# Small transfers on SyncE's queue, Fourier preparation over more slots, and weight decodes asked for earlier, in a one-core attention and MLP kernel

## The chip, the cores and the metric

The kernel runs on one core of a Trainium2 chip. The core has five engines that run side by side, each through its own instructions in order: TensorE (PE in the profile, with its weight loads as PEld), VectorE (DVE), ScalarE (ACT), GpSimd (POOL) and SyncE (SP), which only issues transfers. The metric is the device time of one execution in microseconds (us), lower is better.

## What is computed

Three layers, one behind the other, in float32:

```python
# 1: causal attention with a decay, 4 batches x 8 heads, 576 positions, 64 wide
scores = scale * q @ k^T;  cum = cumsum(log(clip(f)))
scores = where(causal, -1e9, scores + cum[:, None] - cum[None, :])
attn = exp(scores - max);  x = (attn / sum(attn)) @ v          # (4, 576, 512)
# 2: Fourier mixing and an MLP
u = x + real(fft(fft(x, axis=seq), axis=channel))
u = u + relu(norm(u) @ w_ch1) @ w_ch2                           # 512 -> 2048 -> 512
# 3: a second mixing
theta = u @ w_theta;  zr, zi = u * cos(theta), u * sin(theta)
u = u + w_tok_r @ zr + w_tok_i @ zi
out = u + relu(u @ w_ch)
```

The weights of layers 2 and 3 are stored as 64-bit integers and are decoded on the chip into a high and a low float32 part; each product is a sum of three matmuls (high by high, high by low, low by high).

## The kernel before, in words

**Attention (phase 1).** A loop over slots n = -2 to 32, one head a slot. A slot has four quarters q = 0 to 3, and each quarter takes one step of several generators, in a fixed order that is the order of the program on every engine: `least_units` of head n+2 (row minima of the scores; PE L216, L217, L221, DVE L224), `weight_units` of head n (scores again and the exponential: PE L253 to L258, ACT L259), `least_end` of head n+1 in quarter 1 (PE transposes the minima, L234, ACT writes them to `mr`, L236, two transfers put them into row 66 of `q2`), `av_units` of head n-1 (PE L270 into the bank `pt`, of which there is one), `prep_units` of head n+3 (ACT L191, L196, POOL L192, L200, DVE L202, and a transfer of two rows into `kl`), then `rows` (`pair_units`: for each two heads the division by the sums), `norm`, `fft` (`fft_units`: the Fourier transform of one batch, after each eight slots) and `early` (`stash_units`: eight weight blocks are decoded and kept in DRAM). At the slot's end ACT copies `pt` to `x` (`evac_head`, L284), and a transfer sends the row of sums to `zt`. The next slot's L270 can write `pt` only after that copy.

**`pair_units`**: DVE takes the reciprocal of `zt` (L294, L295); `zd` (to DRAM) and `R` (back, over 64 partitions, 288 KB) are two transfers on SP; DVE and POOL multiply `x` by `R` into `XB` and `XA` (L303, L310); a row goes out and another in (L306 to L314); `E` and `O` are their sum and difference (L318, L319). There are three `x` buffers, so the copy of one head waits until `XA` has read the head three before.

**`fft_units`**: the inputs are folded and split into high and low parts (`xx`, `ee`, `oo`, `xh`, `xl`, `eh`, `el`, `oh`, `ol`: L338 to L355), which is called the Fourier preparation here; then six groups of matmuls with an ACT copy and a DVE difference each, then the sums back into `u`.

**MLP (phase 2).** 96 units (g, c, k): four groups g of four weight blocks, six chunks c of 384 positions, four blocks a chunk. Unit n issues `ffn1` of unit n+2 (12 matmuls, L737, ACT L742, DVE L743) and then `ffn2` of unit n (L751). After each quarter of `ffn2`, `later` takes a step of the norm of a later chunk and one step of a decode (`fill`). A decode has six steps: the transfer of a raw block (L543), ACT L563 and L564, DVE L566 and L567, DVE L571 and ACT L576, DVE L578 and POOL L579, POOL L581 and L582. At most two raw blocks are held, and a decode's first step comes eight ticks after its transfer. A block that is needed before its decode is done is finished on the spot (`finish`). The table `todo` says after which unit a block's decode is asked for. In group 3 the 18 blocks of `wtk` for layer 3 are decoded.

**Layer 3 (phase 3)** begins with the chain PE L931, DVE L937 to L955, ACT L948 to L956, POOL L957, on which the matmuls L967 wait.

Transfers are issued by the engine whose name stands in the call: `nc.sync` is SP's queue, `nc.scalar` is ACT, which issues between its own instructions.

## Time and profile before

| | before |
|---|---|
| median of 3 runs | 1139.08 us (1138.71 to 1142.91) |
| profiled execution | 1138.91 us, of which the span from first to last instruction is 1137.1 us |
| busy over the span | PE 90%, PEld 79%, DVE 54%, POOL 45%, ACT 36% |
| mean granted TensorE clock | 0.938 |
| moved by transfers | 81.43 MB, 72 GB/s on average |

The profile is that of one execution. PE is busy for nine tenths of the span, so what the other engines do counts only where PE waits for it, or where PE runs at the lower of its two clock levels (granted clock 0.5, which is 1.2 of 2.4 GHz). A busy share says nothing about that; the waits, the stages and the clock do.

### The profile page before, as it was taken

The page shows a single profiled execution, that of the slowest core. Times are in us where ns is not written, and L with a number is a line of the kernel's source. Part 1 is how long each engine was busy: PE and PEld are TensorE (multiplying, and loading weights), DVE is VectorE, ACT ScalarE, POOL GpSimd, SP SyncE. Part 2 cuts the span into 40 slices and gives each one's busy share as a digit, 9 for nine tenths or more (in the row PEclk, how much of TensorE's full clock was granted, in tenths as well). Part 3 has the DMA queues.
Part 4 walks back from the last instruction along what each step waited for, and adds up shares of the span by engine and source line. Part 5 has one row for each costly group of instructions (what it writes and reads, how often), then busy time and mean ns, then how long its engine had stood idle before and what let it go on. Part 6 is the DMA issues. An engine that isn't in the chain of part 4 may idle for free.

```text
span 1137.1 us, 16339 instructions
## 1 busy us (share of the span) xinstructions
PE 1018.5 (90%) x6112; PEld 903.5 (79%) x6112; DVE 608.6 (54%) x1260; ACT 409.0 (36%) x861; POOL 512.4 (45%) x515
## 2 busy tenths in 40 slices
PE   4998798879989889878799979997999699999998
PEld 2765575647757677778799969996999699999998
DVE  7465656553655554445533534353446766665654
ACT  3454542423443422232322322232233543443422
POOL 5355645362543532454514534353345854444431
PEclk9998898867989988999999989998999799999999
DMA  3463432432220400110212212122341100000001
GB/s 114 130 190 121 166 121 71 134 117 65 86 94 23 159 12 1 37 38 37 75 38 70 79 56 93 67 82 75 116 137 43 42 1 12 32 11 33 12 32 42
DMA packets 33130, 81.43 MB, mean 72 GB/s; under 512 B 9238, under 2 KB 12694, under 8 KB 33052
## 3 DMA queue, kind: packets, MB, share of 16 engines
q1 hardware_dynamic: 26084, 75.87, 20.1%
q0 software_dynamic: 2288, 3.06, 1.2%
q10 hardware_dynamic: 4680, 1.47, 0.6%
q8 instruction: 48, 0.79, 0.3%
q14 instruction: 30, 0.25, 0.1%
HBM read 66.87 MB, written 13.36 MB: 71 GB/s over the span
## 4 chain that ended last, share of the span: by engine, by line
PE 59%; DVE 12%; POOL 8%; ACT 4%; issue 3%; DMA 3%; ACTq 0%; SPq 0%; POOLq 0%; DVEq 0%
PE pa L737 16%; PE pb L751 8%; PE po L751 6%; PE pt L270 4%; PE pb L967 4%; PE pa L978 4%; PE pa L931 3%; PE po L967 2%; PE pa L216 2%; PE pb L253 1%; PE pb L374 1%; PE pb L402 1%; PE pa L217 1%; PE pb L254 1%; POOL a L579 1%
## 5 line engine op out<-in xcount | busy, mean ns | idle before, releaser
L737 PE MATMUL pa<-un,wf 128*128 128x384 f32 x1152 | 228.6, 345 | 31.0 <-ACT wf L576 14.0
L737 PEld LDWEIGHTS pa<-un,wf 128*128 128x128 f32 x1152 | 206.5, 193 | 38.9 <-ACT wf L576 15.0
L743 DVE SCALAR_TENSOR_TENSOR h<-pa,h 128x384 fp32r<-128x384 f32 x96 | 53.5, 557 | 196.4 <-ACT h L742 196.2
L270 PE MATMUL pt<-PT,v 128*65 128x320 f32 (+4 forms) x448 | 122.2, 395 | 22.4 <-ACT x L284 22.4
L751 PE MATMUL pb<-h,wf 128*128 128x384 f32 x636 | 132.7, 341 | 1.4 <-DVE u L759 1.4
L224 DVE TENSOR_REDUCE mn<-pa 128x1 f32<-128x512 f32 (+2 forms) x192 | 84.7, 471 | 79.9 <-PE pa L221 75.1
L742 ACT ACTIVATE h<-pa 128x384 fp32r<-128x384 f32 x96 | 46.9, 490 | 192.1 <-PE pa L737 191.4
L751 PEld LDWEIGHTS pb<-h,wf 128*128 128x128 f32 x636 | 113.5, 190 | 3.1 <-DVE u L759 1.7
L967 PE MATMUL pb<-wtk,z 128*128 128x288 f32 x540 | 99.9, 298 | 10.8 <-ACT z L956 7.7
L216 PE MATMUL pa<-hi 128*128 128x512 f32 (+2 forms) x192 | 93.9, 489 | 16.3 <-ACT mn L156 12.3
L751 PE MATMUL po<-h,wf 128*128 128x384 f32 x492 | 106.8, 347 | 0.0
L259 ACT ACTIVATE PT<-pb 128x512 f32<-128x512 f32 (+1 forms) x128 | 63.7, 500 | 103.0 <-PE pb L256 75.9
L957 POOL TENSOR_TENSOR z<-kra,z 128x256 fp32r<-128x256 f32 x72 | 54.2, 771 | 86.2 <-ACT z L956 86.2
L967 PEld LDWEIGHTS pb<-wtk,z 128*128 128x128 f32 x540 | 82.8, 191 | 11.9 <-ACT z L956 7.9
L579 POOL TENSOR_TENSOR a<-a,wf 128x512 f32<-128x512 f32 x24 | 30.8, 1286 | 135.0 <-DVE t L578 120.7
L751 PEld LDWEIGHTS po<-h,wf 128*128 128x128 f32 x492 | 90.8, 196 | 0.0
L270 PEld LDWEIGHTS pt<-PT,v 128*65 128x65 f32 x448 | 57.5, 152 | 34.9 <-ACT x L284 24.4
L192 POOL TENSOR_TENSOR hi<-raw,hi 64x576 fp32r<-64x576 f32 x31 | 44.3, 1429 | 85.9 <-ACT hi L191 73.7
L217 PE MATMUL pa<-kl,q 66*128 66x512 f32 (+2 forms) x192 | 71.2, 372 | 12.9 <-issue 4.9
L253 PE MATMUL pb<-hi 128*128 128x512 f32 (+2 forms) x192 | 73.4, 389 | 0.3 <-DVE ea L411 0.3
L967 PE MATMUL po<-wtk,z 128*128 128x288 f32 x324 | 70.1, 299 | 0.0
L216 PEld LDWEIGHTS pa<-hi 128*128 128x128 f32 x192 | 42.2, 220 | 33.7 <-issue 18.4
(202 smaller groups left out, 2048.9 us busy)
## 6 DMA issues: line engine op xcount, KB each, us to landing
raw<-in_qk SPq DMA_DIRECT2D x31, 576.0 KB
raw<-in_wf SPq DMA_DIRECT2D x32, 512.0 KB
v<-in_vp SPq DMA_DIRECT2D x16, 325.0 KB
raw<-in_wtk SPq DMA_DIRECT2D x18, 288.0 KB
R<-zd SPq DMA_DIRECT2D x16, 288.0 KB
st_wf<-raw SPq DMA_DIRECT2D x8, 512.0 KB
wf<-st_wf SPq DMA_DIRECT2D x8, 512.0 KB
out<-ob SPq DMA_DIRECT2D x12, 288.0 KB
```

The source lines that it names most:

```text
L216: nc.tensor.matmul(out, hi[:, 1, q], hi[:, 0, a:b], start=True, stop=False)
L217: nc.tensor.matmul(out, q2[0:66, q], kl[0:66, a:b], start=False, stop=not diag)
L224: nc.vector.tensor_reduce(mn[:, col : col + 1], ps[:, off : off + b - a], mybir.AxisListType.X, ALU.min)
L253: nc.tensor.matmul(out, hi[:, 0, k], hi[:, 1, a:b], start=True, stop=False)
L259: nc.scalar.activation(PT[:, 512 * bank : 512 * bank + w], ps[:, 0:w], AF.Exp, scale=-0.125)
L270: nc.tensor.matmul(T[:65, 256 + a : 256 + hi_q], v[:, j, g, :], PT[:, PTOFF[j] + a - 128 * j : PTOFF[j] + hi_q - 128 * j], start=j == 0, s ...
L737: nc.tensor.matmul(ps[:, 0:CH], t[:, l, 128 * d : 128 * d + 128], un[r][:, d], start=n == 0, stop=n == 11)
L742: nc.scalar.activation(h[:, 0], ps[:, 0:CH], AF.Relu)
L743: nc.vector.scalar_tensor_tensor(h[:, 1], ps[:, 0:CH], 0.0, f(h[:, 0]), ALU.max, ALU.subtract)
L751: nc.tensor.matmul(outs[d], t[:, l, 128 * d : 128 * d + 128], h[:, r], start=k % G == 0 and n == 0, stop=k % G == G - 1 and n == 2,)
L957: nc.gpsimd.tensor_tensor(z[:, 1], t, f(z[:, 0]), ALU.subtract)
L967: nc.tensor.matmul(acc[k][th], z[:, l, 128 * k : 128 * k + 128], self.wtk[kt][:, r, 288 * th : 288 * th + 288], start=first and i == 0 and ...
```

## The change

Three parts, by what the code does:

1. The four small transfers of the attention that ACT issued (`kl`, two of `mr`, `zt`) are issued by SP. The two of `mr` come a quarter later, the one of `zt` in the next slot's first quarter (`send_sums`).
2. `pair_units` and `fft_units` have their steps in more quarters (two pairs can be under way, `chains`); the last pairs and transforms of batches 2 and 3 take fewer (`tight`). Copies `yh` and `zh` go from ACT to DVE, one difference (`ol`) from POOL to DVE. The early decode takes 12 quarters a block in place of nine.
3. In phase 2 the decodes of a group are asked for at its start, five steps are taken a unit in place of four, and in group 3 eight in place of six, with a wait of six ticks in place of eight.

```diff
-            nc.scalar.dma_start(f(kl[64:66]), f(self.scr[n]))
+            nc.sync.dma_start(f(kl[64:66]), f(self.scr[n]))
...
-        nc.scalar.dma_start(f(q2[66:67, 0:512]).rearrange("o (i s) -> o i s", i=4), f(mr[0:4]))
-        nc.scalar.dma_start(f(q2[66:67, 512:576]), f(mr[4:5, 64:128]))
+        yield
+        nc.sync.dma_start(f(q2[66:67, 0:512]).rearrange("o (i s) -> o i s", i=4), f(mr[0:4]))
+        nc.sync.dma_start(f(q2[66:67, 512:576]), f(mr[4:5, 64:128]))
...
-        nc.scalar.copy(x, T[:65, 256:832])
-        nc.scalar.dma_start(zt[64 * g : 64 * g + 64, :], x[64:65, :].rearrange("o (p c) -> o p c", c=9))
+        self.nc.scalar.copy(hd["x"], T[:65, 256:832])
+    def send_sums(self, hd, zt):
+        self.nc.sync.dma_start(zt[64 * g : 64 * g + 64, :], hd["x"][64:65, :].rearrange("o (p c) -> o p c", c=9))
...
+        self.send_sums(hds[1], zt)
-        for _ in range(2):
+        for _ in range(1 if tight else 2):
             yield
         nc.vector.tensor_scalar(zt, zt, 1e-9, None, ALU.add)
         nc.vector.reciprocal(zt, zt)
+        if not tight:
+            yield
         nc.sync.dma_start(zd, zt)
+        if not tight:
+            yield
...
-        for _ in range(4):
+        for _ in range(3):
             yield
         nc.vector.tensor_tensor(XB[p : p + 64, t, :], hds[1]["x"][0:64], R[:, 1], ALU.mult)
+        nc.gpsimd.tensor_tensor(XA[p : p + 64, t, :], hds[0]["x"][0:64], R[:, 0], ALU.mult)
+        if not tight:
+            yield
...
-        for _ in range(9):
+        for _ in range(6 if tight else 11):
             yield
...
         nc.vector.tensor_tensor(ee[:, :, 1:288], E[:, :, 1:288], E[:, :, 575:288:-1], ALU.add)
         nc.vector.tensor_copy(ee[:, :, 0:289:288], E[:, :, 0:289:288])
+        yield
         nc.scalar.copy(eh, ee)
-        yield
         nc.vector.tensor_tensor(oo[:, :, 0:287], O[:, :, 1:288], O[:, :, 575:288:-1], ALU.subtract)
+        nc.vector.tensor_copy(xx[:, 0:289:288], x256[:, 0:289:288])
+        yield
         nc.scalar.copy(oh, oo)
+        nc.scalar.copy(xh, xx)
...
-        nc.gpsimd.tensor_tensor(ol, oo, f(oh), ALU.subtract)
+        nc.vector.tensor_tensor(ol, oo, f(oh), ALU.subtract)
...
-            nc.scalar.copy(yh[:me, s, :], ps[:me, 0:258])
+            nc.vector.tensor_copy(yh[:me, s, :], ps[:me, 0:258])
...
-        for _ in range(4 if w is self.w2 else 1):
+        for _ in range(3 if w is self.w2 else 1):
             yield
...
-            if self.queue and self.ticks - self.born[self.queue[0]] >= 8:
+            if self.queue and self.ticks - self.born[self.queue[0]] >= self.age:
...
-        for j, (c, k) in enumerate([[1, 3], [2, 3], [4, 2], [4, 3]]):
+        for j, (c, k) in enumerate([[1, 3], [1, 3], [4, 2], [4, 2]]):
             at(0, c, k, load, 4 + j)
         for g in (1, 2):
-            for j, (c, k) in enumerate([[0, 1], [1, 3], [3, 1], [4, 3]]):
-                at(g, c, k, load, G * g + 4 + j)
+            for j in range(4):
+                at(g, 0, 1, load, G * g + 4 + j)
         for j in range(4):
-            at(1, j, 2, self.keep_big, "wth", j)
-            at(2, j, 2, self.keep_big, "wch", j)
+            at(1, 0, 1, self.keep_big, "wth", j)
+            at(2, 0, 1, self.keep_big, "wch", j)
...
-            self.fill(2 if g == 3 and d % 2 else 1)
+            self.fill(2 if g == 3 or d == 1 else 1)
...
+            if g == 3:
+                self.age = 6
```

What the change does to the order on the engines is shown at three places. Lines of the changed kernel are up to 31 higher (L260 is L259 before, L585 is L563, L600 is L576, L771 is L742).

The first is ACT in slot 11, in which the preparation of the first Fourier transform stands; before:

```order
L259 ACTIVATE PT<-pb 128x512
L190 DMA kl_105<-scr 2x576
L191 CAST hi<-raw 128x576
L259 ACTIVATE PT<-pb 128x512
L236 ACTIVATE mr<-pa 5x128
L237 DMA q_99<-mr 1x4x128
L238 DMA q_99<-mr 1x16x4
L196 ACTIVATE hi<-raw 128x576
L342 CAST xh<-xx 1x290
L259 ACTIVATE PT<-pb 128x512
L349 CAST eh<-ee 128x580
L259 ACTIVATE PT<-pb 128x64
```

and in the changed kernel, a slot later, where its preparation stands:

```order
L260 ACTIVATE PT<-pb 128x512
L191 CAST hi<-raw 128x576
L260 ACTIVATE PT<-pb 128x512
L236 ACTIVATE mr<-pa 5x128
L196 ACTIVATE hi<-raw 128x576
L357 CAST eh<-ee 128x580
L260 ACTIVATE PT<-pb 128x512
L361 CAST oh<-oo 128x576
L362 CAST xh<-xx 1x290
L260 ACTIVATE PT<-pb 128x64
L283 COPY x<-pt 65x576
```

The three transfers are gone from ACT, and the copy of `xx`, which depends on the longest chain, went from first to last of the three.

The second is SP in one even slot and the odd one behind it, where before it had:

```order
L296 DMA zd<-zt 128x9
L298 DMA R<-zd 64x1152
L181 DMA raw<-in_qk 128x1152
L587 DMA st_wf_1_1014<-raw 128x1024
L306 DMA rb<-XB 1x576
L314 DMA XB<-rb 1x576
L543 DMA raw<-in_wf 128x1024
L181 DMA raw<-in_qk 128x1152
L176 DMA v<-in_vp 128x650
```

and now, from `R` on to the next `zd`:

```order
L305 DMA R<-zd 64x1152
L238 DMA q_102<-mr 1x4x128
L239 DMA q_102<-mr 1x16x4
L614 DMA st_wf_0_800<-raw 128x1024
L181 DMA raw<-in_qk 128x1152
L176 DMA v<-in_vp 128x650
L190 DMA kl_105<-scr 2x576
L316 DMA rb<-XB 1x576
L287 DMA zt<-x 64x1x9
L565 DMA raw<-in_wf 128x1024
L325 DMA XB<-rb 1x576
L238 DMA q_99<-mr 1x4x128
```

SP's queue now has the small transfers between the large ones (`R`, the raw blocks, the stores `st_wf`), ahead of some and behind others.

The third is ACT at the end of group 1 of phase 2. L742 is the activation of one `ffn1`; what stands between two of them is the decodes' share of one unit. Before:

```order
L742 ACTIVATE h<-pa 128x384 x3
L563 ACTIVATE a<-raw 128x512
L564 ACTIVATE t<-raw 128x512
L576 CAST wf<-a 128x512
L742 ACTIVATE h<-pa 128x384
L563 ACTIVATE a<-raw 128x512
L564 ACTIVATE wf<-raw 128x512
L576 CAST wf<-a 128x512
L563 ACTIVATE a<-raw 128x512
L564 ACTIVATE wf<-raw 128x512
L576 CAST wf<-a 128x512
L742 ACTIVATE h<-pa 128x384
```

and now:

```order
L771 ACTIVATE h<-pa 128x384 x3
L585 ACTIVATE a<-raw 128x512
L586 ACTIVATE t<-raw 128x512
L585 ACTIVATE a<-raw 128x512
L586 ACTIVATE t<-raw 128x512
L771 ACTIVATE h<-pa 128x384
L600 CAST raw<-a 128x512 x2
L771 ACTIVATE h<-pa 128x384 x7
```

Before, two decodes of the block that the next `ffn1` reads stand whole between two activations; now the last weight block (tile `wf`) was decoded ten units earlier, the last rows are blocks for layer 3 (tile `raw`), and seven units follow with no decode.

## Rows read from the trace of the kernel before

**Rows 1.** Stages by windows: phase 1, its end to group 1, groups 1 to 3, layer 3's start.
```profile
core 0: us, PE busy (x) PEld busy (x) DVE busy (x) ACT busy (x) POOL busy (x), PEclk, DMA share, GB/s
45.80:392.80 347.00, 307.25 (x1741) 218.42 (x1741) 196.26 (x399) 147.41 (x301) 170.14 (x149) 0.89 0.36 111
392.80:545.50 152.70, 132.22 (x694) 120.21 (x694) 71.19 (x142) 44.59 (x93) 63.10 (x59) 0.93 0.10 37
545.50:884.70 339.20, 314.08 (x1753) 311.43 (x1753) 156.01 (x311) 100.65 (x200) 144.63 (x130) 0.96 0.25 80
884.70:912.00 27.30, 17.41 (x115) 16.55 (x114) 20.09 (x48) 13.79 (x36) 22.84 (x32) 0.75 0.07 22
```

**Rows 2.** Waits of PE over the span: us in total, times, longest us.
```profile
PE pt L270 <- ACT x L284: 22.4, 13, 3.5
PE pa L737 <- ACT wf L576: 14.0, 3, 5.6
...
PE pa L737 <- POOL wf L582: 9.7, 3, 3.8
PE pb L967 <- ACT z L956: 7.7, 1, 7.7
```

**Rows 3.** Windows, columns as in rows 1: first chunk of each group, and a quiet one.
```profile
545.50:571.50 26.00, 19.28 (x98) 18.63 (x98) 14.56 (x22) 6.68 (x12) 15.79 (x12) 0.87 0.27 82
571.50:588.20 16.70, 16.70 (x98) 16.70 (x97) 6.97 (x15) 4.96 (x10) 0.00 (x0) 1.00 0.08 28
655.20:683.70 28.50, 19.98 (x99) 19.15 (x98) 11.33 (x23) 7.39 (x13) 10.60 (x9) 0.82 0.19 56
...
768.60:796.70 28.10, 19.59 (x98) 18.77 (x97) 10.94 (x22) 7.40 (x13) 10.18 (x9) 0.82 0.24 76
```

**Rows 4.** The page's group of POOL's first decode operation, L579, in phase 2.
```profile
L579 POOL TENSOR_TENSOR a<-a,wf 128x512 f32<-128x512 f32 x24 | 30.8, 1286 | 135.0 <-DVE t L578 120.7
```

**Rows 5.** Windows: a quiet slot, the three preparation slots, and the stretch behind the second.
```profile
53.30:60.80 7.50, 7.50 (x50) 5.50 (x50) 3.64 (x12) 4.05 (x8) 3.58 (x4) 1.00 0.77 222
126.60:141.60 15.00, 9.43 (x52) 6.05 (x50) 10.16 (x20) 6.69 (x13) 10.89 (x11) 0.82 0.41 146
224.90:242.40 17.50, 9.80 (x54) 6.31 (x52) 13.99 (x23) 5.91 (x13) 11.11 (x12) 0.80 0.17 55
323.20:337.40 14.20, 9.60 (x54) 6.15 (x53) 8.79 (x19) 5.49 (x11) 7.14 (x9) 0.89 0.22 67
242.40:277.70 35.30, 34.33 (x138) 25.12 (x139) 11.82 (x28) 11.95 (x27) 9.23 (x9) 0.57 0.29 86
```

**Rows 6.** Timeline of ACT in the first preparation slot: start, us, idle before and releaser.
```profile
135.71 0.43 ACT L342 CAST xh<-xx 1x290 fp32r<-1x290 f32 x1 [3.19 <-DVE xx L341]
...
138.81 0.68 ACT L349 CAST eh<-ee 128x580 fp32r<-128x580 f32 x1 [2.18 <-DVE ee L348]
```

**Rows 7.** Timeline of ACT in slot 5 (q marks the issue of a transfer).
```profile
82.46 0.66 ACTq L237 DMA_DIRECT2D q<-mr  x1
83.17 0.53 ACTq L238 DMA_DIRECT2D q<-mr  x1
83.74 0.68 ACT L196 ACTIVATE hi<-raw 128x576 fp32r<-128x576 f32 x1 [1.31 <-issue]
```

**Rows 8.** ACT's groups in phase 1: the first of the early decode's two conversions.
```profile
L563 ACT ACTIVATE a<-raw 128x512 f32<-128x512 f32 x8 | 5.3, 666 | 0.0
```

**Rows 9.** Timelines: SP's `zd` and the `R` that waits for it; PE's reader of `mr`.
```profile
77.31 0.33 SPq L296 DMA_DIRECT2D zd<-zt  x1
78.92 0.46 SPq L298 DMA_DIRECT2D R<-zd  x1
...
86.88 0.39 PE L254 MATMUL pb<-q,kl 67*128 67x512 f32 x1
```

**Rows 10.** Timelines: one `R` on SP, and DVE's reader of it.
```profile
198.26 0.46 SPq L298 DMA_DIRECT2D R<-zd  x1
...
202.11 0.75 DVE L303 TENSOR_TENSOR XB<-x,R 64x576 f32<-64x576 f32 x1 [0.35 <-DMA R<-zd]
```

More of the change, by code (lines that the diff above doesn't have):

```diff
@@ L309, in pair_units @@
             nc.sync.dma_start(self.x256, row)
-        nc.gpsimd.tensor_tensor(XA[p : p + 64, t, :], hds[0]["x"][0:64], R[:, 0], ALU.mult)
+        if not tight:
+            yield
         if h == 0:
@@ L319, in pair_units, with fft_units @@
             nc.gpsimd.tensor_tensor(O[:, t, :], XA[:, t, :], XB[:, t, :], ALU.subtract)
-        yield
-    def fft_units(self, b, E, O, rows):
+    def fft_units(self, b, E, O, rows, tight):
         nc = self.nc
         w = self.c1
-        for _ in range(9):
+        for _ in range(6 if tight else 11):
             yield
@@ L339, in fft_units @@
         nc.gpsimd.memset(xx[:, 288:290], 0.0)
-        nc.gpsimd.tensor_tensor(xx[:, 1:288], x256[:, 1:288], x256[:, 575:288:-1], ALU.add)
-        nc.vector.tensor_copy(xx[:, 0:289:288], x256[:, 0:289:288])
-        nc.scalar.copy(xh, xx)
-        nc.gpsimd.tensor_tensor(xl, xx, f(xh), ALU.subtract)
         nc.gpsimd.memset(ee[:, :, 288:290], 0.0)
         nc.gpsimd.memset(oo[:, :, 286:288], 0.0)
+        nc.gpsimd.tensor_tensor(xx[:, 1:288], x256[:, 1:288], x256[:, 575:288:-1], ALU.add)
         yield
@@ L348, in fft_units @@
         nc.vector.tensor_copy(ee[:, :, 0:289:288], E[:, :, 0:289:288])
+        yield
         nc.scalar.copy(eh, ee)
+        nc.vector.tensor_tensor(oo[:, :, 0:287], O[:, :, 1:288], O[:, :, 575:288:-1], ALU.subtract)
+        nc.vector.tensor_copy(xx[:, 0:289:288], x256[:, 0:289:288])
         yield
-        nc.vector.tensor_tensor(oo[:, :, 0:287], O[:, :, 1:288], O[:, :, 575:288:-1], ALU.subtract)
         nc.scalar.copy(oh, oo)
+        nc.scalar.copy(xh, xx)
         nc.gpsimd.tensor_tensor(el, ee, f(eh), ALU.subtract)
         yield
-        nc.gpsimd.tensor_tensor(ol, oo, f(oh), ALU.subtract)
+        nc.vector.tensor_tensor(ol, oo, f(oh), ALU.subtract)
+        nc.gpsimd.tensor_tensor(xl, xx, f(xh), ALU.subtract)
         yield
-        if b < B - 1:
+        if not tight:
             yield
@@ L385, in fft_units @@
                 nc.tensor.matmul(ps[:mo, 0:256], l, r, start=k == 0, stop=k == 5)
-            nc.scalar.copy(zh[:mo, s, :], ps[:mo, 0:256])
+            nc.vector.tensor_copy(zh[:mo, s, :], ps[:mo, 0:256])
             nc.vector.tensor_tensor(zl[:mo, s, :], ps[:mo, 0:256], f(zh[:mo, s, :]), ALU.subtract)
@@ L488, in phase1 @@
                 if q == 1 and 0 <= n + 1 < NH:
-                    self.least_end(heads[n + 1])
+                    e = self.least_end(heads[n + 1])
+                if q > 0:
+                    next(e, 0)
                 next(c, 0)
                 next(prep, 0)
-                next(rows, 0)
+                if q == 0 and sums:
+                    self.send_sums(*sums)
+                    sums = None
+                for r in chains:
+                    next(r, 0)
                 next(norm, 0)
@@ L502, in phase1 @@
             if m >= 0:
-                self.evac_head(heads[m], T, zt)
-                if g == 1:
-                    for _ in rows:
-                        pass
-                    rows = self.pair_units(h, (heads[m - 1], heads[m]), zt, XA, XB, E, O, zd, rb)
+                self.evac_head(heads[m], T)
+                b = p // NP
+                tight = b > 1 and h == NP - 1
+                if g == 0:
+                    sums = (heads[m], zt)
+                else:
+                    rows = self.pair_units(h, (heads[m - 1], heads[m]), zt, XA, XB, E, O, zd, rb, tight)
+                    chains.append(rows)
                     if h == NP - 1:
@@ L510, in phase1 @@
                             pass
-                        fft = self.fft_units(p // NP, E, O, rows)
+                        fft = self.fft_units(b, E, O, rows, tight)
+        for _ in chains[0]:
+            pass
         pinned.close()
@@ L575, in decode @@
             self.nraw -= 1
+        if w is self.w2:
+            yield
         nc.scalar.copy(hi, a)
@@ L586, in decode @@
             self.stash[keep] = self.sdram.tile([128, 2, n], F32R, name=name)
+            if w is self.w2:
+                yield
+                yield
             nc.sync.dma_start(f(self.stash[keep]).rearrange("p t n -> p (t n)"), f(flat[:, 0 : 2 * n]))
+            if w is self.w2:
+                yield
         yield
@@ L642, in fill @@
                     self.queue.insert(min(self.active - 1, len(self.queue)), g)
-                    if self.ticks - self.born[self.queue[0]] < 8:
+                    if self.ticks - self.born[self.queue[0]] < self.age:
                         self.queue.remove(g)
@@ L660, in p2_open @@
         self.active = 3
-        self.born, self.ticks = {}, 0
+        self.born, self.ticks, self.age = {}, 0, 8
         for k in range(G):
@@ L684, in norm_units @@
         nc.gpsimd.tensor_tensor(s1, s1, s2, ALU.add)
-        for _ in range(2):
+        for _ in range(3):
             yield
```

15 lines of the change are left out of this document (7 added, 8 removed).

## The prediction, made before the changed kernel ran

> **What bounds the kernel now.** I read the stages first, then the waits of PE, then single slots and units. In the stages [rows 1] the column to read is PE's busy time against the window's length, with the granted clock beside it. Phase 1 takes 347.0 us with PE busy 307.25, so PE waits for 39.75 us of it. Its clock is 0.89, and since the clock has the two levels 0.5 and 1.0, it stood at half for 0.22 x 347 = 76 us. Part of that half-clock time is idle already counted; I take 60 of the 76 us as busy, and half of that, 30 us, as lost. So phase 1 loses about 70 us to waits and to the clock that they bring down. The stretch behind it loses 20.5 us of waiting in 152.7, groups 1 to 3 lose 25.1 us of waiting at a clock of 0.96, and the start of layer 3 waits 9.9 of its 27.3 us. Against these stands the rest of the span, where PE is busy at full clock. PE is the bound, and what can be won is its waits and its half-clock stretches.
>
> The waits say who is late [rows 2]. The largest in phase 1 is L270 behind ACT's copy of `pt`: 22.4 us in 13 waits. In phase 2 three waits for a cast (14.0 us) and three for POOL's last decode operation (9.7 us) stand before an `ffn1`: few and long. One wait of 7.7 us stands at layer 3's start.
>
> The three pairs in phase 2 lie at the group changes [rows 3]. A quiet chunk of 98 matmuls takes 16.70 us; the first chunks of groups 1, 2 and 3 take 26.00, 28.50 and 28.10 with the same 98. That is 9.3 + 11.8 + 11.4 = 32.5 us, the half clock (0.87, 0.82, 0.82) included.
>
> In phase 1 the worst slots are those with a Fourier preparation [rows 5]. A quiet slot takes 7.5 us; these take 15.0, 17.5 and 14.2 with nearly the same matmuls (52 to 54 against 50, for which I allow 0.2 us each slot). The excess is 46.7 - 3 x 7.7 = 23.6 us. Behind the second, 35.3 us run at a clock of 0.57: 86% of it, 30 us, at half, with PE busy for almost all of it, so about 15 us more. Why ACT is late there is seen in its timeline [rows 6]: it stands 3.19 us before the copy of `xx` and 2.18 us before that of `ee`, both waiting for DVE, and the exponentials and the copy of `pt` are queued behind.
>
> **The change part by part.** The sum is made against the profiled execution, 1138.91 us (1137.1 us of span and 1.8 us around it), which is 0.2 us under the median shown.
>
> *Decodes asked for at a group's start, five steps a unit.* In the order on ACT the last two decodes of group 1 stood whole between two activations, so an `ffn1` waited for all their steps. They now stand ten units ahead of it, and what is last are blocks that only layer 3 needs. Groups 2 and 3 then begin without a wait: -11.8 and -11.4 us. In group 1 the blocks can't be asked for earlier than before chunk 4, since their buffers open there; the last one's cast stands just before its `ffn1`. Behind a cast come three POOL operations of 1.29 us [rows 4], 3.9 us, with about 1.5 us for the activation, the cast and a vector operation ahead of them; PE has half a unit of cover, 2.1 us (a unit is 16.70 / 4 [rows 3]). I leave 3.5 us there, with a little half clock: -5.3 in place of -9.3. Together **-28.5 us**. Bounds: -32.5 if that one goes as well, -20 if denser decodes cost DVE and POOL time elsewhere (POOL's 1.29 us three times for each decode, 5 of 6 steps a unit, is 3.2 us of 4.2).
>
> *Eight steps a unit in group 3, six ticks.* Before, four of the eighteen `wtk` decodes remain when `ffn1` has ended, and ACT, DVE and POOL do them inside the first chain of layer 3. In the changed order only the casts of the last two remain. Layer 3's start loses 9.9 us of waiting and, at a clock of 0.75, about 3 us more [rows 1]. The chain itself still has to run once, for which I leave 3 us: **-10 us**, bounds -13 and -4.
>
> *The Fourier preparation over more quarters.* Each ACT copy now stands a quarter, 1.9 us of a 7.5 us slot, behind the DVE or POOL operation that it reads; the waits there are 3.19 and 2.18 us [rows 6], so most of each is covered. ACT also loses the `yh` and `zh` copies to DVE, which was waiting for them. The excess of the three slots and the half clock behind the second is 23.6 + 15 = 38.6 us. I take three quarters of it, **-29 us**, since DVE and POOL operations in these slots are also stretched. Bounds: -38 and -10.
>
> *Transfers off ACT.* The two issues of `mr` take 0.66 and 0.53 us, and ACT's next operation had 1.31 us of idle before it [rows 7]; the other two transfers cost at most as much each, so ACT gets back up to 2.6 us of a 7.5 us slot. With that the copy of `pt` is less late, and the pair division, the decodes' POOL operations and the stores on SP no longer meet in one quarter. The rest of phase 1's loss is 70 - 38.6 = 31 us, spread over some ten waits with different releasers. I take two fifths: **-13 us**. Bounds: -25 and 0.
>
> *A wait that is added.* The early decode now has a fixed rhythm of three slots, and its two conversions on ACT, L563 and L564, always stand in the last quarter, just ahead of the copy of `pt` for which PE waits. Each takes 0.67 us [rows 8] (I take the second as long). About 0.5 us of the 1.3 is covered by what PE does before L270; eight blocks make 8 x 0.8 = **+6 us**. Bounds: 0, and +14 if the raw block is not there yet either, since its transfer is issued in the first quarter of the same slot.
>
> *The small transfers behind the large ones.* `mr` is issued by 83.70 at the latest before [rows 7] and read at 86.88 [rows 9], 3.2 us later. A small transfer's issue to its release of the next takes 1.6 us (77.31 to 78.92 [rows 9]), so 1.6 us are left over. On SP, `R` or a raw block or both may be ahead of it. A quiet slot moves 222 GB/s with the 16 engines busy for 0.77 [rows 5], so 288 GB/s at full; the 288 + 512 KB of both are 2.8 us, about at the margin, and they come together in four slots. I cost this at 0; bounds 0 and +12. The Trainium skill (DMA: Bandwidth & Descriptors, Queues, rings and completion order) says that an engine takes turns between queues, but works through one queue in order. By that rule `mr` gives up its turn beside the bulk when it leaves ACT's queue, and the sum would get the +12; no row here shows it, since ACT issued `mr` in every slot.
>
> *`R` a quarter later.* Its reader now comes three quarters, 5.6 us, behind its issue, where one `R` took 3.85 us (198.26 to 202.11 [rows 10]). Cost 0; what it hides behind is the slot's own matmuls. If it came 1 us late in each of sixteen pairs, `XA` and with it the copy of `pt` would be late, +16.
>
> *The stretch from 392.8 to 545.5.* The transform of batch 3 starts a few steps earlier, and the decodes meet the norms as before: -2 us, bounds -10 and +8.
>
> Sum: -28.5 - 10 - 29 - 13 + 6 - 2 = -76.5. 1138.9 - 76.5 = **1062 us**. With each term at its own distance from the bounds the sum moves by some 20 us either way, so the forecast's own range is 1040 to 1084.
>
> **The rivals.**
>
> *Phase 1 gives little back.* Stalls of this phase have many releasers (for L270, in 13 waits, never over 3.5 us), and taking away one uncovers the next; the added wait and late `R` come in. Then the decode parts stay, -38.5 us, and phase 1 nets nothing: 1100 us. For it: DVE and POOL have the most work in just these slots (13.99 and 11.11 of 17.5 us [rows 5]). Against it: ACT has 2.6 us a slot more.
>
> *More goes than I take.* If phase 1's other waits mostly vanish too and the clock stays up, another 25 us: 1037 us.
>
> *SP's queue becomes the bound: slower.* SP works in order; a transfer that waits for DVE or POOL (`zd`, the stores) holds `mr` behind it, and with `mr` the scores of the next slot. It decides when PE loses 76.5 / 30 = 2.6 us in each of 30 slots, so when `mr` lands 2.6 + 1.6 = 4.2 us later than before. At 3 us a slot, +90: 1152 us. For it: six small transfers a slot now share a queue with up to three large ones. Against it: each of them is placed behind its source by a quarter or more.
>
> *It does not do what it says.* Engines other than PE already carry the decodes with little room, so that asking earlier only moves the waits into the units, and phase 1's waits into other quarters: 1130 to 1140 us. Against it: in the quiet chunk [rows 3] POOL does nothing and DVE 6.97 of 16.70 us.
>
> **How the numbers follow.** Forecast 0.60; little from phase 1 0.18; more than I take 0.11; slower 0.06; nothing 0.05. About 0.5% (6 us) is what a measurement of this kernel can tell from no change. Faster by more than that: 0.60 + 0.18 + 0.11 + 0.02 of the last = 0.91; the same 0.03; slower 0.06. The range takes in the forecast, the better case and most of the first rival: 1032 to 1104 us, 0.60 + 0.11 + 0.12.
>
> **What would show it.** In the profile after: no wait of an `ffn1` for a cast or POOL at the second and third group change, and chunks of 16.7 us there; one short one at the first. L967's wait at layer 3's start at about 3 us. Preparation slots near 9 us, and no 30 us at half clock behind the second. ACT's idle before L196 gone. L270's waits behind the copy of `pt` left mainly in the eight slots with L563 and L564 in the last quarter. I would be wrong if L254 waits for `mr` in many slots, if POOL's `XA` waits for `R` each pair, or if phase 2's units each grow beyond 4.2 us.

## The result and the profile after

The changed kernel takes 1092.78 us (median of 4 runs, 1088.11 to 1093.09) beside 1140.99 us for the kernel before on the same chip (4 runs, 1138.71 to 1148.19): a ratio of 0.956, 95% interval 0.951 to 0.961. The prediction was 1062 us with a range of 1032 to 1104. The direction and the range held; the gain was 48 us where 76.5 had been summed. The medians and ranges below leave out executions more than 1.5% above the fastest of their kernel.

The stages of the changed kernel, by windows with the columns and the order of [rows 1]:

```profile
45.30:377.60 332.30, 305.05 (x1762) 218.82 (x1761) 211.19 (x423) 140.56 (x286) 170.97 (x149) 0.91 0.40 122
377.60:527.50 149.90, 128.28 (x672) 114.97 (x673) 77.32 (x148) 41.26 (x83) 59.48 (x56) 0.94 0.07 24
527.50:850.43 322.93, 310.80 (x1753) 308.02 (x1752) 166.62 (x327) 105.09 (x213) 154.96 (x142) 0.98 0.26 86
850.43:865.90 15.47, 13.82 (x109) 13.37 (x108) 11.87 (x30) 8.72 (x21) 13.13 (x20) 1.00 0.01 2
```

The stages shrank by 14.7, 2.8, 16.3 and 11.8 us; together 45.6 of the 46.1 us by which the span did (1137.1 to 1091.0). Phase 1 hides something here, since the big layers' first `ffn1` runs inside its window: it starts at 360.8 us instead of 389.1, 28.3 us earlier, but the second chunk only at 389.1 instead of 405.0, 15.9 us earlier. So 12.4 us were won and given back within one chunk.

PE's waits over the span, as in [rows 2] (L271 was L270, L766 was L737, L998 was L967, L780 is `ffn2`):

```profile
PE pt L271 <- ACT x L283: 7.4, 10, 1.7
PE pb L732 <- POOL s L727: 6.6, 4, 2.5
...
PE pa L766 <- POOL wf L606: 4.9, 1, 4.9
PE po L780 <- ACT x L283: 4.9, 1, 4.9
PE po L780 <- ACT h L771: 4.3, 2, 2.9
...
PE pa L766 <- ACT wf L600: 1.9, 1, 1.9
...
PE pb L255 <- DMA q<-mr: 1.6, 1, 1.6
PE pb L998 <- ACT z L987: 1.5, 1, 1.5
```

The copy of `pt` costs a third of what it did, and the casts and POOL operations ahead of `ffn1` are down from three each to one. Two rows are new: `ffn2` waits 4.9 us for a copy of phase 1, and 4.3 us for its own activation `h`.

The first chunks of groups 1, 2 and 3, with a quiet one third, as in [rows 3]:

```profile
527.50:553.80 26.30, 19.14 (x98) 18.18 (x97) 11.29 (x20) 6.65 (x12) 15.43 (x12) 0.87 0.23 80
637.60:659.40 21.80, 18.75 (x97) 18.18 (x96) 7.75 (x16) 5.07 (x10) 7.68 (x6) 0.92 0.35 116
659.40:676.10 16.70, 16.70 (x99) 16.70 (x98) 7.15 (x15) 5.42 (x10) 2.52 (x2) 1.00 0.17 56
742.70:761.50 18.80, 17.28 (x97) 16.70 (x97) 7.75 (x16) 5.08 (x10) 7.71 (x6) 1.00 0.31 107
```

Group 1 begins no better than before (26.00), group 2 wins 6.7 us and group 3 9.3, and both still stand 5.1 and 2.1 us over a quiet chunk.

The slots with a Fourier preparation (the first, second and fifth row), the slots behind the second and the third, in which the last of the preparation and the first of the transform now lie (third and sixth), and the stretch behind the second pair (fourth), columns as in [rows 5]:

```profile
136.40:148.00 11.60, 8.91 (x53) 6.23 (x52) 11.50 (x15) 5.35 (x11) 10.41 (x8) 0.90 0.42 127
219.60:228.90 9.30, 7.28 (x48) 5.09 (x46) 9.16 (x17) 5.88 (x14) 5.96 (x5) 1.00 0.38 98
228.90:242.20 13.30, 12.66 (x63) 9.40 (x64) 7.96 (x20) 3.89 (x8) 7.57 (x7) 0.74 0.32 110
242.20:277.50 35.30, 34.68 (x222) 25.25 (x220) 26.20 (x54) 13.43 (x27) 16.49 (x12) 1.00 0.31 93
299.50:308.50 9.00, 8.01 (x51) 5.46 (x50) 8.90 (x15) 5.61 (x11) 6.29 (x5) 1.00 0.32 104
308.50:327.10 18.60, 15.48 (x80) 11.46 (x80) 11.06 (x23) 3.94 (x9) 9.67 (x9) 0.72 0.14 46
```

The preparation slots take 11.6, 9.3 and 9.0 us, near the 9 that was expected (15.0, 17.5 and 14.2 before). The third's gain moved on, since the slot behind it takes 18.6 us where it took 11.2; with the slot behind each, the six take 73.8 us, against 88.1 before. The stretch behind the second pair does 222 matmuls at full clock where 138 ran at 0.57 before.

### The profile page after: what moved, and what is told of

Read it like the earlier page. It is cut to its first block, busy times and chain, and to the rows that moved or that the text cites. A ratio compares the mean times of both kernels' runs of the same rounds, so it can differ in the third digit from the quotient of the medians.

```text
span 1091.0 us, 16375 instructions
## 1 busy us (share of the span) xinstructions
PE 1005.8 (92%) x6112; PEld 892.5 (82%) x6112; DVE 631.1 (58%) x1288; ACT 398.3 (37%) x837; POOL 511.1 (47%) x511
## 5 line engine op out<-in xcount | busy, mean ns | idle before, releaser
L766 PE MATMUL pa<-un,wf 128*128 128x384 f32 x1152 | 229.6, 345 | 18.7 <-ACT un L751 5.3
L766 PEld LDWEIGHTS pa<-un,wf 128*128 128x128 f32 x1152 | 205.0, 192 | 29.0 <-ACT un L751 9.6
L780 PE MATMUL pb<-h,wf 128*128 128x384 f32 x636 | 131.1, 340 | 0.6 <-DVE u L788 0.6
L271 PE MATMUL pt<-PT,v 128*65 128x320 f32 (+4 forms) x448 | 118.7, 386 | 7.6 <-ACT x L283 7.4
L260 ACT ACTIVATE PT<-pb 128x512 f32<-128x512 f32 (+1 forms) x128 | 64.3, 504 | 168.0 <-PE pb L257 141.1
L771 ACT ACTIVATE h<-pa 128x384 fp32r<-128x384 f32 x96 | 46.9, 490 | 197.6 <-PE pa L766 197.4
L780 PEld LDWEIGHTS pb<-h,wf 128*128 128x128 f32 x636 | 113.3, 190 | 1.6 <-DVE u L788 1.3
L780 PE MATMUL po<-h,wf 128*128 128x384 f32 x492 | 105.5, 344 | 9.6 <-ACT x L283 4.9
L998 PE MATMUL pb<-wtk,z 128*128 128x288 f32 x540 | 98.2, 295 | 2.3 <-ACT z L987 1.5
L780 PEld LDWEIGHTS po<-h,wf 128*128 128x128 f32 x492 | 89.5, 193 | 11.5 <-ACT x L283 5.2
L998 PEld LDWEIGHTS pb<-wtk,z 128*128 128x128 f32 x540 | 81.5, 188 | 2.9 <-ACT z L987 1.7
L603 POOL TENSOR_TENSOR a<-a,wf 128x512 f32<-128x512 f32 x24 | 31.3, 1306 | 96.7 <-DVE t L602 96.7
L271 PEld LDWEIGHTS pt<-PT,v 128*65 128x65 f32 x448 | 56.3, 149 | 18.5 <-ACT x L283 9.5
L998 PE MATMUL po<-wtk,z 128*128 128x288 f32 x324 | 69.0, 294 | 0.0
```

Source lines behind the costliest of these rows:

```text
L260: nc.scalar.activation(PT[:, 512 * bank : 512 * bank + w], ps[:, 0:w], AF.Exp, scale=-0.125)
L271: nc.tensor.matmul(T[:65, 256 + a : 256 + hi_q], v[:, j, g, :], PT[:, PTOFF[j] + a - 128 * j : PTOFF[j] + hi_q - 128 * j], start=j == 0, s ...
L766: nc.tensor.matmul(ps[:, 0:CH], t[:, l, 128 * d : 128 * d + 128], un[r][:, d], start=n == 0, stop=n == 11)
L771: nc.scalar.activation(h[:, 0], ps[:, 0:CH], AF.Relu)
L780: nc.tensor.matmul(outs[d], t[:, l, 128 * d : 128 * d + 128], h[:, r], start=k % G == 0 and n == 0, stop=k % G == G - 1 and n == 2,)
L998: nc.tensor.matmul(acc[k][th], z[:, l, 128 * k : 128 * k + 128], self.wtk[kt][:, r, 288 * th : 288 * th + 288], start=first and i == 0 and ...
```

## Where the lost part of the gain went, in the trace

The end of phase 1, by timelines of SP, ACT, DVE, POOL and PE in the changed kernel:

```profile
354.19 0.35 SPq L301 DMA_DIRECT2D zd<-zt  x1
356.29 9.50 SPq L620 DMA_DIRECT2D wf<-st_wf  x8
365.83 0.50 SPq L287 DMA_DIRECT2D zt<-x  x1
366.38 0.62 SPq L305 DMA_DIRECT2D R<-zd  x1
...
375.51 0.75 DVE L310 TENSOR_TENSOR XB<-x,R 64x576 f32<-64x576 f32 x1 [1.03 <-DMA R<-zd]
375.55 1.96 POOL L311 TENSOR_TENSOR XA<-x,R 64x576 f32<-64x576 f32 x1 [6.49 <-DMA R<-zd]
377.55 0.64 ACT L283 COPY x<-pt 65x576 f32<-65x576 f32 x1 [3.66 <-POOL XA L311]
378.24 2.29 PE L780 MATMUL po<-h,wf 128*128 128x384 f32 x6 [4.87 <-ACT x L283]
```

Read it upwards. `ffn2` waits for the copy that frees its PSUM bank; the copy waits for `XA`, which still reads the buffer of `x`; `XA` waits for `R`; and `R` is issued behind eight fetches of 512 KB and lands 9.1 us after its issue, where the one in [rows 10] took 3.85. The Trainium skill (DMA: Bandwidth & Descriptors, Queues, rings and completion order) says that a DMA engine works through the descriptors of one queue in order; the 9.1 us agree, and run e5 tests it. `R` is also issued late, 12.2 us behind `zd`, and part of that is a wait that stands ahead of it on SP: the second of the fetches waits for DVE, by SP's waits from 354 to 367 us:

```profile
SPq L620 <- DVE un L752: 5.8, 1, 5.8
```

Before, `R` was issued ahead of the fetches (379.83 and 382.16 us).

Group 2's first chunk, by timelines of ACT and PE:

```profile
634.70 0.67 ACT L585 ACTIVATE a<-raw 128x512 f32<-128x512 f32 x1 [6.84 <-DMA raw<-in_wth]
...
641.10 0.66 ACT L585 ACTIVATE a<-raw 128x512 f32<-128x512 f32 x1 [5.17 <-DMA raw<-in_wth]
...
642.21 0.48 ACT L771 ACTIVATE h<-pa 128x384 fp32r<-128x384 f32 x1
642.74 1.21 PE L780 MATMUL po<-h,wf 128*128 128x384 f32 x3 [2.90 <-ACT h L771]
```

A decode's conversion stands at the head of ACT's order with its raw block not there. SP had issued that load late (637.38), because it waited for the store of the kept block that used the buffer before (issued at 630.38). Behind the conversion on ACT is the activation that `ffn2` needs.

## The experiments

Of all kernels below those whose orders agree up to there tell how much one execution of phase 1 varies. From the third copy of `pt` to the 31st it takes 290 to 305 us in six traces of the changed order (296.9, 291.0, 290.2, 305.1, 296.3, 293.0) and 323.2 and 329.1 in two of the order before. A phase-1 difference under some 10 us in one trace therefore proves nothing. The experiments ran on other chips than the result; the kernel before took 1139.73 to 1145.17 us there, so a difference to the changed kernel of under some 5 us isn't told by the medians, and where the ratio intervals overlap (e3, e5, e6, e7) the trace has to decide.

**e1: the decodes alone.** In the kernel before:

```
-for j, (c, k) in enumerate([[1, 3], [2, 3], [4, 2], [4, 3]]):
+for j, (c, k) in enumerate([[1, 3], [1, 3], [4, 2], [4, 2]]):
...
-self.fill(2 if g == 3 and d % 2 else 1)
+self.fill(2 if g == 3 or d == 1 else 1)
```

> The kernel before with the decode scheduling of the big layers alone (where loads and keeps are asked for, two steps of decode at d == 1, age 6 in the last group); phase 1 as before. Theory A, the two halves of the change are independent and add: group changes about -16 us and the start of layer 3 about -12 us, so about 1140 - 28 = 1112 us, with layer 3's start at clock 1.0. Theory B, part of the gain of the decodes needs the earlier phase 1 (a clock that is not pulled down, queues that are free): the gain is 20 us or less, 1120 us or more.

Measured: 1116.67 us beside 1139.73, ratio 0.980 (0.976 to 0.984), 23 us. The first chunks take 27.1, 20.1 and 18.9 us (1.1 us lost, 8.4 and 9.2 won, 16.5 in all, against 15.7 in the full change), and layer 3's start, from its first matmul to the next batch of L933 behind L969, takes 15.8 us as in the full change, against 26.4 before. In these stages the decode parts are worth what they are worth in the full change. The time lies between the two theories; this execution's phase 1 was 6 us longer than that of the kernel before, with the same order.

**e2: phase 1 alone.** The same lines put back in the changed kernel.

> The changed kernel with the decode scheduling of the big layers put back to the old one; transfers, preparation and pair division as changed. Theory A (they add): about -18 us, so about 1122 us, group 1 starts near 527 us and the first-chunk stalls of the groups are those of before (7.3 and 10.3, 9.9 and 10.2, 9.9 and 9.8 us units). Theory B: phase 1 alone gives 25 us or more, 1115 us or less, and the new decode order costs something in the stretch before group 1.

Measured: 1132.51 us, ratio 0.992 (0.988 to 0.997), 7 us. So the halves don't add: 23 + 7 is 30, not 48, and neither theory gave this. The missing 18 us stand in one stretch, from chunk 1 of group 0 to group 1, by windows of e2 and of the changed kernel:

```profile
384.40:540.70 156.30, 133.46 (x624) 119.97 (x625) 72.95 (x141) 38.09 (x78) 54.22 (x52) 0.84 0.06 21
```
```profile
389.10:527.50 138.40, 117.50 (x624) 104.50 (x625) 75.22 (x143) 38.12 (x78) 54.85 (x52) 0.96 0.07 24
```

The same 624 matmuls are busy for 133.5 us at a clock of 0.84 and for 117.5 at 0.96; waiting differs by 2 us only (22.8 and 20.9). Behind it are longer single waits, by the waits of PE in that stretch of e2 and of the changed kernel:

```profile
PE pb L732 <- POOL s L727: 12.9, 4, 5.0
```
```profile
PE pb L732 <- POOL s L727: 6.6, 4, 2.5
```

In e2 two POOL operations of a decode (L603, 1.27 us each) stand between the normalisation's sums. A stretch at half clock begins in or at the end of each of the two waits of 5 us and lasts 10.2 and 6.8 us. That is a third of the 50 us that a clock of 0.84 makes in 156.3 us (11 us at 0.96 in the changed kernel), so these waits account for a part only; what starts the rest isn't shown. The change also has one step more ahead of the mean's matmul in the normalisation, which the diff ahead of the prediction doesn't show; e10 takes it out.

**e3: only `mr` back on ScalarE's queue.**

```
-nc.sync.dma_start(f(q2[66:67, 0:512])...)
-nc.sync.dma_start(f(q2[66:67, 512:576]), f(mr[4:5, 64:128]))
+nc.scalar.dma_start(f(q2[66:67, 0:512])...)
+nc.scalar.dma_start(f(q2[66:67, 512:576]), f(mr[4:5, 64:128]))
```

> The changed kernel with only the two mr rows sent from ScalarE's queue again, in the same quarter. Theory A, the mr rows wait behind the bulk transfers of SyncE's queue (R, raw) and that starts the half clock at 70 us: the 1.6 us wait of L255 for q<-mr goes, the 17 us at half clock from 70.5 us shrink to 7 or less, and the kernel is 4 to 10 us faster than the changed one (1083 to 1089). Theory B, the copy of pt, late behind the decode's conversions on ScalarE (1.05 us at 71.2 us), starts it: the wait of L255 goes but the half clock stays, and the time moves by less than 3 us.

Measured: 1097.32 us, ratio 0.963 (0.960 to 0.967): no gain. L255 waits for `mr` 3.9 us in five waits, against 1.6 in one. Theory A falls, and the wait doesn't go, as both theories had it. The long half clock at 70 us, on which both rested, doesn't belong to the order: the slot takes 13.2, 8.9, 8.8, 13.2, 11.1 and 11.3 us in the six traces of the same order. By windows, in the changed kernel and in e2:

```profile
71.20:84.40 13.20, 12.53 (x45) 8.89 (x46) 5.21 (x14) 4.32 (x10) 4.16 (x5) 0.50 0.34 75
```
```profile
72.50:81.30 8.80, 8.13 (x45) 5.74 (x46) 4.38 (x12) 4.32 (x10) 3.72 (x5) 0.81 0.37 88
```

**e4: the early decode's conversions behind the copy of `pt`.**

```
-for _ in range(3 if w is self.w2 else 1):
+for _ in range(4 if w is self.w2 else 1):
...
-    yield
     yield
 nc.sync.dma_start(f(self.stash[keep])...)
```

> The changed kernel with the early decode's two conversions a quarter later (four yields after the raw load, one fewer ahead of the store, so the same 12 quarters a block): they follow the copy of pt instead of standing ahead of it. Theory A (the copy waits behind conversions that wait for raw, the prediction's added wait): the copy-to-copy times of the slots in which a block starts drop by about 1 us each plus the half clock at 70 us, so 6 to 12 us less than the changed kernel (1081 to 1087). Theory B, mr behind the bulk transfers is what starts the half clock: 3 us or less.

Measured: 1103.07 us (1101.71 to 1114.06, three executions), ratio 0.971 (0.965 to 0.977), 10 us slower than the changed kernel. Both theories fall: PE's waits for the copy grow. The waits between the third copy of `pt` and the 31st, first in e4, then in the changed kernel (ACT's for `XA`, PE's for the copy):

```profile
ACT x L283 <- POOL XA L311: 21.2, 7, 4.9
...
PE pt L271 <- ACT x L283: 18.8, 11, 2.6
```
```profile
ACT x L283 <- POOL XA L311: 11.8, 6, 3.8
...
PE pt L271 <- ACT x L283: 7.4, 10, 1.7
```

In the five other traces of the changed order these waits are 12.0 to 13.3 and 6.7 to 9.6 us, so the growth is clear of chance. The copy is late here behind `XA` on POOL, whose buffer it overwrites: in three pairs of e4 the decode's last POOL operation stands directly ahead of `XA`, in the changed kernel in none. With it the edit moved the whole decode, and what the two conversions alone cost ahead of the copy isn't shown. Nor is every late copy behind `XA`: in e11 and e12 PE waits 20 us for the copies and ACT 8 for `XA`.

**e5: the eight fetches behind `R`.** The loads move from the opening of the big layers' pools to the quarter after the sums and `R`:

```
-for k in range(G):
-    self.load(k)
...
 next(fft, 0)
+if n == NH and q == 0:
+    for k in range(G):
+        self.load(k)
```

> The changed kernel with the eight fetches wf<-st_wf of the last slot of phase 1 issued behind R of the pair before the last, instead of ahead of it (the first fetch about 2.5 us later). Theory A (the fetches on SyncE's queue hold up R, whose reader XA holds up the copy that closes phase 1): R lands before 362 us on the changed kernel's scale instead of 375.5, the 4.9 us wait of the first ffn2 matmul for ACT x goes, with the half clock behind it, and the time falls by 5 to 12 us (1081 to 1088). Theory B (the first ffn1 units are bound by the normalisation and by the fetches themselves, which now come later): the first ffn1 waits 2 to 3 us more for wf and the time moves by less than 3 us.

Measured: 1083.04 us (1078.15 to 1093.92), ratio 0.952 (0.943 to 0.961), 9.7 us less than the changed kernel. By timelines of SP, ACT and POOL:

```profile
351.29 0.54 SPq L305 DMA_DIRECT2D R<-zd  x1
351.93 6.69 SPq L623 DMA_DIRECT2D wf<-st_wf  x8
...
360.72 0.62 ACT L283 COPY x<-pt 65x576 f32<-65x576 f32 x1
...
361.87 1.41 POOL L311 TENSOR_TENSOR XA<-x,R 64x576 f32<-64x576 f32 x1
```

`XA` waits for nothing any more and PE's wait behind the last copy is gone. From the first `ffn1` to the second chunk 17.6 us pass, against 28.3: 10.7 us. The nine other kernels in which `R` stays behind the fetches take 27.0 to 29.9 us there, so this is clear of chance, and theory A holds. `ffn1` waits 4.5 us for `wf` in place of 1.0, as theory B had it, and the chunk is shorter all the same.

**e6: a faster decode at the end of group 0.**

```
-if g == 3:
-    self.age = 6
+self.age = 5 if g == 0 and c > 3 else 6 if g == 3 else 8
...
-self.fill(2 if g == 3 or d == 1 else 1)
+self.fill(2 if g == 3 or d == 1 or 20 <= n < 24 and d == 3 else 1)
```

> The changed kernel with age 5 instead of 8 for the decodes in chunks 4 and 5 of group 0 and one more step of decode a unit (at d == 3) in chunk 5, so that blocks 6 and 7 are decoded two units earlier. Theory A (the first chunk of group 1 waits for decodes that began late, because the second pair of raw loads is asked for only when the first is half done): its unit times 6.85 and 11.04 us fall to 4.2 to 5, so 7 to 9 us less (1084 to 1086). Theory B (GpSimd and VectorE are the bound there, and more steps only shift the wait into chunk 5): chunk 5 grows by 5 us or more and the time moves by less than 3 us.

Measured: 1096.78 us, ratio 0.963 (0.955 to 0.970); the time shows no gain. By windows, chunk 5 of group 0 and the first of group 1:

```profile
517.50:538.10 20.60, 19.04 (x97) 18.22 (x98) 10.51 (x20) 6.67 (x13) 3.80 (x5) 0.92 0.07 27
538.10:560.40 22.30, 19.08 (x97) 18.15 (x97) 9.48 (x16) 5.44 (x10) 13.77 (x11) 0.92 0.19 70
```

The first chunk of group 1 falls by 4.0 us, between the theories; 5.6 us over a quiet chunk stay. The chunk before it is 1.4 us longer than in the changed kernel (19.2), but not by this edit: e4 and e11, which don't have it, take 20.6 and 20.5 us there, and e8, which has it, 19.2. The profiled execution's phase 1 was 8 us longer, which covers the gain in its time.

**e7: seven more steps of age for a raw load behind a kept block.**

```
-self.born[g] = self.ticks
+self.born[g] = self.ticks + (7 if self.held else 0)
+self.held = max(self.held - 1, 0)
```

with `held` raised by one for each kept block of the big layers.

> The changed kernel in which a raw load asked for just after a keep block is stored gets 7 steps more before its conversions may start. Theory A (ScalarE's conversion L585 stands at the head of its queue, waiting for a raw load that itself waits for the store, and holds up relu): the first unit of group 2 falls from 8.9 to about 5 us or less and that of group 3 from 6.3 to about 4.2, so 4 to 7 us less (1086 to 1089). Theory B (those units wait for something else, such as the DMA queue or the weights): they stay within 1 us of what they were.

Measured: 1089.52 us, ratio 0.957 (0.949 to 0.966), 3 us less than the changed kernel. By windows, the first chunks of groups 2 and 3:

```profile
635.80:652.50 16.70, 16.70 (x97) 16.70 (x97) 6.78 (x15) 4.23 (x8) 7.68 (x6) 1.00 0.19 64
735.80:752.60 16.80, 16.80 (x98) 16.80 (x98) 8.48 (x16) 5.37 (x10) 4.87 (x4) 1.00 0.23 80
```

Both are as quiet as any: 5.1 and 2.0 us, all that the prediction had still to get there. For the two units theory A holds. But part of it is given back later, in the fourth chunk of group 3, which takes 16.7 us in the changed kernel:

```profile
786.00:805.30 19.30, 17.61 (x99) 16.66 (x98) 12.44 (x27) 7.95 (x20) 13.47 (x17) 1.00 0.44 142
```

POOL is busy for 13.47 us of it, and `ffn2` waits 1.4 us for DVE's `u`; e8, which has this edit, takes 19.2 us there, and no other kernel more than 16.8.

**e9: all small transfers back on ScalarE's queue, behind their sources** (the `dma_start` of `kl`, `mr` and `zt` from `nc.sync` to `nc.scalar`, `mr` and `zt` a quarter earlier).

> The changed kernel with all three kinds of small transfers of phase 1 (row kl, row mr, sums zt) sent again from ScalarE's queue right behind their sources; preparation, pair division and decodes as changed. Theory A, the transfers are worth the 13 us that the prediction gave them: the kernel is 8 to 14 us slower than the changed one (1101 to 1106). Theory B, nearly all of phase 1's gain is from the spread preparation and division, and the queue counts for little: within 4 us of the changed kernel (1089 to 1097), the last pair's sums perhaps gaining what they lost behind the fetches.

Measured: 1104.07 us, ratio 0.970 (0.962 to 0.978), 11.3 us slower than the changed kernel: theory A. In the profiled execution (1108.87 us, 16.1 more) 7.6 us stand in the stretch before group 1 (146.0 us at a clock of 0.86, against 138.4 at 0.96); from the third copy of `pt` to the 31st it takes 300.8 us, within the 290 to 305 of the changed order, so no loss is shown in phase 1's slots. `R` is late here too, by SP's timeline:

```profile
362.82 9.46 SPq L615 DMA_DIRECT2D wf<-st_wf  x8
372.32 0.48 SPq L304 DMA_DIRECT2D R<-zd  x1
```

From the first `ffn1` to the second chunk 29.4 us pass, as many as in the changed kernel. What put `R` behind the fetches is therefore not the small transfers on SP; what remains are the added quarters in `pair_units`.

**e10: e2 with the normalisation's extra step taken out.**

```
-for _ in range(3):
+for _ in range(2):
     yield
 ps = self.bank_b()
 nc.tensor.matmul(ps[:, 0:CH], self.mean, s1, start=True, stop=True)
```

> The kernel with phase 1 changed and the big layers' decodes as before (156.3 us from chunk 1 of group 0 to group 1, against 140.5 before and 138.4 in the changed kernel), with the one extra step ahead of the mean's matmul in the normalisation taken out again. Theory A (the extra step puts the normalisation's squares beside the old decode steps, two L603 on GpSimd ahead of L727): that stretch returns to 138 to 143 us, the kernel takes 1116 to 1121. Theory B (the later last pair and its Fourier chain fill the engines there): the stretch stays at 152 us or more, 1128 or more.

Measured: 1131.15 us (1120.09 to 1136.12, six executions), ratio 0.992 (0.987 to 0.997). The stretch falls to 142.6 us at 0.92, as theory A said, and the time doesn't, as theory B said: phase 1 from the third copy to the 31st took 304 us here, 13 more than in e2 and still within the 290 to 305, with two waits of L271 (2.9 and 2.7 us) among the last slots, where the first two normalisations run. Whether the extra step is what pays there, or chance, stays open.

**e11: the Fourier units as before.** Nine quarters ahead of them (six for the tight pairs as in the change), fewer `yield`s between their steps, and:

```
-nc.vector.tensor_tensor(ol, oo, f(oh), ALU.subtract)
+nc.gpsimd.tensor_tensor(ol, oo, f(oh), ALU.subtract)
...
-nc.vector.tensor_copy(yh[:me, s, :], ps[:me, 0:258])
+nc.scalar.copy(yh[:me, s, :], ps[:me, 0:258])
```

> The changed kernel with the Fourier units written as before (fewer quarters between the steps of the preparation, the rounded halves of the sums on ScalarE, o's residue on GpSimd); pair division, transfers and decodes as changed. Theory A (the spread preparation is worth the 29 us of the prediction): 20 to 30 us slower than the changed kernel, 1112 to 1122, with the preparation slots back at 14 to 17 us. Theory B (the division spread over more slots and the transfers made most of phase 1's gain): 10 us slower or less, 1103 or less.

Measured: 1104.58 us, ratio 0.969 (0.963 to 0.974), 11.8 us slower than the changed kernel. That is a little over theory B's bound and far from theory A's 20 to 30. The preparation slots, by windows:

```profile
125.80:138.00 12.20, 8.04 (x49) 5.61 (x49) 8.19 (x18) 5.67 (x13) 6.68 (x9) 0.91 0.20 48
217.40:231.00 13.60, 9.31 (x49) 6.29 (x49) 8.66 (x16) 6.42 (x14) 7.94 (x9) 0.87 0.38 122
295.50:309.30 13.80, 8.19 (x51) 5.79 (x51) 8.62 (x18) 5.33 (x12) 8.58 (x10) 1.00 0.39 128
```

They are not back at theory A's 14 to 17 us, and with the slot behind each the six take 73.1 us (with 325 matmuls), against 73.8 (with 363) in the changed kernel and 88.1 before: most of the fall there goes without this edit. Again 7.6 us stand in the stretch before group 1 (146.0 us at 0.88).

**e12: e9 and e11 together.**

> The changed kernel with both the small transfers of phase 1 on ScalarE's queue right behind their sources and the Fourier units written as before; only pair division, the early decode's steps and the decodes of the big layers stay changed. Undone singly the two cost 11 and 12 us. Theory A (each stands in for the other, so that undoing one shows little): together they cost clearly more than the 23 us of the sum, 1122 us or more, and from the third to the 31st copy of pt takes 318 us or more (before 323, changed 290 to 305). Theory B (they add, and the rest of phase 1's gain lies in the division and the early decode): 1112 to 1120 us, and that stretch takes 300 to 312.

Measured: 1111.81 us (1107.88 to 1118.77), ratio 0.971 (0.966 to 0.975), 19 us slower than the changed kernel (15 when each is set against the kernel before on its own chip), under the sum of 23. In time they don't stand in for each other: theory A falls, and the result lies at the edge of theory B. From the third copy to the 31st the profiled execution, the slowest of the four, takes 312 us, against a mean of 295 with the change and 326 before, so about half of what the slots gained remains without these two edits. Against that mean e9 and e11 lose 5 and 4 us in the slots and e12 17, so there it stays open. No run undoes the pair division or the early decode's steps alone; that they carry the rest of the gain is by elimination.

**e8: e5, e6 and e7 together.**

> The changed kernel with the fetches behind R, the faster decodes at the end of group 0 and the hold after a keep block together. Theory A (the three give-backs are separate: 11, 4 and 7 us in the traces of the single edits): 22 us less than the changed kernel, 1068 to 1076 us. Theory B (an earlier stage end only moves a wait on): 12 us less or smaller, 1081 or more.

Measured: 1078.39 us (6 runs, 1075.21 to 1085.96) beside 1140.74, ratio 0.947 (0.942 to 0.952): 14.4 us less than the changed kernel, between the two theories. All three give-backs are gone from the trace as in the single runs: the first `ffn1` to the second chunk takes 17.5 us, and the first chunks of groups 1 to 3 take 22.30, 16.70 and 16.80 us. What is missing of the 22 us is in part e7's new cost: the fourth chunk of group 3 takes 19.2 us. The spans of the two profiled executions differ by 17.6 us (1091.0 and 1073.4). This is the best version of the study.

## Why the prediction was right in sign and 31 us too low

- **Decodes at the group changes**, -28.5 predicted, +0.3 - 6.7 - 9.3 = -15.7 measured. The reading of the order was right, that blocks move ahead by ten units. For groups 2 and 3 the step that failed is "what is last are blocks that only layer 3 needs ... begin without a wait": those blocks still hold ACT's order, and their raw loads wait for stores. That cost 5.1 and 2.1 us; e7 takes both out and gives 2.5 us back later. For group 1 "I leave 3.5 us there" was mis-sized: 9.6 us stayed. The second pair's conversions begin at 534.4 us, 12.6 behind the first pair's, its POOL operations run from 543.1 to 550.8, and `ffn1` waits 4.9 us for the first block's; e6 shows that more and earlier steps win 4 us of it.
- **Layer 3's start**, -10 predicted, 27.3 to 15.5 us, -11.8 measured by windows that hold 115 and 109 matmuls (to the same matmul 26.4 to 15.8, -10.6), with L998's wait down from 7.7 to 1.5 us and the clock at 1.00. Right.
- **Fourier preparation**, -29 predicted, about -12 by e11, and of that 7.6 us in a later stretch. The excess of those slots did largely go; but e11 takes 73.1 us for them and the slots behind, as the changed kernel does (73.8, with more matmuls). The step that failed is to credit this edit with three quarters of the excess of the slots, while division and early decode, spread over more quarters in the same change, work on the same slots; that it is these two is by elimination.
- **Transfers off ACT**, -13 predicted, about -11 by e9. Right in size, but not shown in the place named for it: of e9's loss 7.6 us stand before group 1, and its slots in phase 1 lie within the spread of the changed order.
- **The added wait**, +6 predicted. Not seen as a cost: ACT waited for the raw block twice in phase 1's slots (3.6 us), and moving the decode so that the conversions follow the copy made the kernel 10 us slower (e4). Ahead of the copy ACT waits longest for `XA`, 11.8 us in six waits, which the term didn't have; what the conversions cost by themselves isn't shown.
- **`mr` behind bulk**, 0 taken, bound +12: one wait of 1.6 us, and e3 wins nothing. Right: the +12 didn't come, nor did the rival in which SP's queue becomes the bound.
- **`R` a quarter later**, 0 taken, bound +16: a miss of 10.7 us (e5), in one pair, behind eight fetches. The sign given for it came half true: `XA` waits for `R` in eight of the sixteen pairs, 21.4 us in all, against four and 7.7 us before; what the seven other waits cost PE isn't shown. The text weighed what stands on SP ahead of `mr` in a slot, and did not do the same for `R` in the last slot, where the fetches are and one of them waits for DVE.
- **The stretch before group 1**, -2 predicted, 140.5 to 138.4 us measured. Right by number only: e2, e9, e11 and e12 take 146 to 156 us there, so its clock of 0.96 is itself something that the whole change keeps; why, stays open.

In sum phase 1 up to the first `ffn1` won 28.3 us where -29 - 13 + 6 = -36 had been summed, and `R` took 12.4 us back within the next chunk, of which e5 restores 10.7; with 12.8 us too much at the group changes and 1.8 more than forecast at layer 3's start, the 31 us are placed in the stages. Within phase 1 the division of the gain among the edits stays open, as said.

## What to carry to other kernels

When a transfer is issued later or on another queue, list for it, in every slot and above all the first and last, what stands ahead of it on that queue and what that waits for; a later `R`, behind one batch of prefetches at a seam, cost 10.7 us here, as much as the queue change won. A decode that is moved out of the way of its own consumer still holds its engine's order; it must not be placed where its load can be late. And terms of a sum that act on the same slots are estimated together, or they are counted twice.

## What was not expected of the hardware

One and the same order of instructions ran its fourth slot in 13.2 us at half clock and in 8.8 us at 0.81, and phase 1's slots in 290 to 305 us. With the clock went two halves of a change that didn't add up: 624 matmuls were busy for 117.5 or 133.5 us, with nearly the same waiting (20.9 and 22.8 us), where, of the waits over 0.7 us, only two were longer.
